# Down-projection of a GeGLU feed-forward by seven block products instead of eight

## The chip, the cores and the metric

The kernel runs on one core of a Trainium2 chip. The metric is the time of one execution on the device in microseconds (us), as the median of several runs. A core has five engines that run side by side, each with an instruction queue of its own: TensorE (PE in the profile; its weight loads are listed apart as PEld), VectorE (DVE), ScalarE (ACT), GpSimd (POOL) and SyncE (SP), which here issues the DMAs. TensorE holds a stationary operand of up to 128x128, streams a moving operand through it, and adds into PSUM, of which a bank holds 128x512 f32. The other operands live in SBUF. [...]

## The reference

One transformer layer: attention against a cached window with 32 query heads, and a feed-forward network (FFN), each with an adaptive layer norm and a gate. x has 2048 rows of 512, the FFN is 1792 wide.

```
mod = (silu(c) @ w_mod).reshape(1, 6, 1, -1)
sa, ca, ga, sb, cb, gb = (mod[:, i] for i in range(6))
h = layernorm(x) * (1 + ca) + sa
x = x + ga * attention(h)
h = layernorm(x) * (1 + cb) + sb
x = x + gb * ((gelu(h @ w_gate) * (h @ w_up)) @ w_down)
```

The last product, `@ w_down`, with its row gate `gb`, is what the change is about: a matrix A = gelu(..) * (..) of 2048x1792 by a matrix of 1792x512.

## The kernel before

**Precision.** Each f32 operand is split into two f16 parts, a high and a low one (`halves`, line 152, on GpSimd: one tensor_scalar and one subtract), and each product is made of three matmuls, high by high, high by low, low by high (`mm3`, line 84; its three matmuls are lines 85, 86 and 87 for every use, so groups are told apart by their tiles). Operands are scaled by powers and norms first, so that f16 holds them.

**Order of the whole.** Attention comes first, in 512 steps t (T = 512) whose order on every engine is written out by hand. In its later half the FFN weights are prepared beside it: loaded, scaled, split and stored to a scratch tensor in HBM (`prep_set` for gate and up, `prep_wd` for down). `sched(pos, (load, steps), ...)` plans a buffer: the load, and at which t its steps run; the buffers of tag `raw` (5) and `rw` (2) turn round. A `store` puts the DMA on SP's queue at the step given. On the same queue go the transposes of p, the softmax output, which attention's product with v needs (`pt<-p`). Then comes the FFN; there only SP's order is written out, and a scheduler chooses the order on the other engines from program order and dependences.

**FFN loops.** The rows are taken in two halves of 1024, each as two blocks of 512. The 1792 features are taken in NP = 7 pairs of 128-wide tiles; n counts pairs over both halves (0 to 13), and q = 2n is the gate, q = 2n + 1 the up product of a pair (NQ = 28). Gate and up are already made by seven block products per q (`product`, line 775; `ORDER` gives their order 1, 2, 6, 7, 5, 4, 3), each of 6 matmuls with a 128x512 moving operand. Their four results are named by (row block, feature tile): `"11"`, `"12"`, `"21"`, `"22"`. For even q, `result` (line 1222) applies gelu; for odd q it multiplies by the up product on VectorE and splits the outcome into f16 parts: a ScalarE copy (line 1230) and a VectorE subtract (line 1231), into tiles of tag `ot`, named `at`.

**Down-projection.** `y_tasks` (line 861) makes one row tile of 128 rows of one pair: two weight tiles x three terms = 6 matmuls with a 128x512 moving operand (the down weights, all 512 columns) and A's parts as stationary operand, into one PSUM bank, tag `acc` (`NACC` = 5 banks, name `py`). VectorE then scales and adds it into the row's accumulator (line 877, `acc<-py,dysc,acc`). Pair n's eight row tiles are queued when q = 2n + 1 is done, and `y_next` takes one after each of four products per q. Each pair's two weight tiles of 256 KB are fetched once per half (line 1504). `f_final` (line 1526) stores a finished row tile and frees its accumulator for one of the second half.

**Weight preparation.** `prep_wd` (line 1316) loads two tiles of w_down, takes a norm, and in `make` multiplies by the row gate (line 1333) and the scale (line 160), splits (lines 156 and 157) and stores two tiles of 256 KB.

## Time and profile before

| what | us |
|---|---|
| median of 3 runs | 1746.65 |
| lowest and highest | 1745.91, 1747.25 |
| the profiled execution, its own time | 1745.58 |
| its span, first to last instruction | 1743.8 |
| VectorE busy over the span | 1467.2 |
| TensorE busy over the span | 1717.1 |
| attention without the FFN's preparation | about 0 to 688 |
| attention with it | about 688 to 1240 |
| the FFN | from about 1240 |

The profile is one execution, recorded by the hardware. Times are in us unless marked ns. A group of instructions is shown with its line, its engine, the operation, what it writes and reads (`out<-in`), the tile's shape, the count, then busy time and the mean duration in ns, and the idle time of the engine just before such instructions, with what ended it. A line of the timeline has the start, the duration, the engine, the line of the kernel, the operation and the count of merged instructions. A line of the waits has the engine and line that waited, what it waited for, the sum in us, how often, and the longest. Records of matmuls overlap: the duration of one holds its way through the array, in which the next has begun.

### The profile page before, as it was taken

The numbers are of one execution on the slowest core, as the hardware profiler recorded it, in microseconds if no ns is written. First come the engines' busy times: TensorE is split into PE (matmuls) and PEld (weight loads), VectorE is DVE, ScalarE is ACT, GpSimd is POOL, SyncE is SP. The second block draws the span as 40 slices with busy tenths as digits, with TensorE's granted clock in tenths as the row PEclk, the third lists the DMA queues.
The fourth block names the chain that finished last, engine by engine and source line by source line (L and its number), as shares of the span: only waits on it lengthen the run. The fifth ranks groups of instructions, "written<-read, shape, count | busy, mean of one in ns | idle before, by whom it ended". The sixth has DMA issues, their size and how long they took to land.

```text
span 1743.8 us, 25747 instructions
## 1 busy us (share of the span) xinstructions
PE 1717.1 (98%) x8002; PEld 783.9 (45%) x8002; DVE 1467.2 (84%) x2544; ACT 1208.9 (69%) x2713; POOL 931.8 (53%) x1137
## 2 busy tenths in 40 slices
PE   7999999999999999999999999999999999999999
PEld 4344444444444444444444444444444444444444
DVE  7888898999988889898898898998875888766676
ACT  6988888888877777688778778788774344434342
POOL 4899768788887844557486486675303323100000
PEclk9999999999999999999999999999999999999999
DMA  6989999999999998899999999999976545352222
GB/s 210 234 190 222 213 229 205 239 215 222 229 197 229 221 202 162 188 213 228 225 209 220 241 213 215 212 223 227 199 160 161 172 113 141 91 190 76 88 76 76
DMA packets 692842, 330.23 MB, mean 189 GB/s; under 512 B 597088, under 2 KB 607584, under 8 KB 692704
## 3 DMA queue, kind: packets, MB, share of 16 engines
q1 hardware_dynamic: 692416, 328.06, 82.5%
q8 instruction: 63, 1.03, 0.3%
q14 instruction: 75, 0.61, 0.1%
q10 hardware_dynamic: 288, 0.52, 0.1%
HBM read 129.63 MB, written 53.61 MB: 105 GB/s over the span
## 4 chain that ended last, share of the span: by engine, by line
PE 88%; DVE 4%; POOL 3%; DMA 2%; ACT 2%; issue 1%; SPq 0%; POOLq 0%; ACTq 0%
PE py L85 9%; PE py L87 9%; PE py L86 9%; PE po L85 6%; PE po L87 6%; PE po L86 6%; PE ps L85 6%; PE ps L87 5%; PE ps L86 5%; PE fa L85 3%; PE fa L86 3%; PE fa L87 3%; PE qa L85 3%; PE qa L87 3%; PE qa L86 3%; DMA pt<-p 2%
## 5 line engine op out<-in xcount | busy, mean ns | idle before, releaser
L929 ACT ACTIVATE ee<-ps,nm 128x512 f32<-128x512 f32 x512 | 350.5, 685 | 243.3 <-DVE nm L920 240.2
L948 DVE SCALAR_TENSOR_TENSOR p<-ee,rr,p 128x512 f16<-128x512 f32 x512 | 456.8, 892 | 2.1 <-ACT p L943 1.9
L920 DVE TENSOR_REDUCE nm<-ps 128x1 f32<-128x512 f32 x512 | 350.4, 684 | 105.1 <-PE ps L87 101.9
L943 ACT ACTIVATE p<-ee,rr 128x512 f16<-128x512 f32 x512 | 363.1, 709 | 10.6 <-DMA pt<-p 9.5
L85 PE MATMUL ps<-k,qt 128*128 128x512 f16 x512 | 193.9, 379 | 5.3 <-ACT ee L929 4.5
L85 PE MATMUL po<-pt,v 128*128 128x512 f16 x512 | 194.0, 379 | 4.1 <-DMA pt<-p 2.4
L87 PE MATMUL po<-pt,v 128*128 128x512 f16 x512 | 194.1, 379 | 1.4 <-POOL v L157 1.4
L87 PE MATMUL ps<-k,qt 128*128 128x512 f16 x512 | 194.0, 379 | 0.6 <-DVE qt L667 0.6
L86 PE MATMUL py<-wo,ot 128*128 128x512 f16 x512 | 194.0, 379 | 0.0
L87 PE MATMUL py<-wo,ot 128*128 128x512 f16 x512 | 194.0, 379 | 0.0
L86 PE MATMUL po<-pt,v 128*128 128x512 f16 x512 | 194.0, 379 | 0.0
L85 PE MATMUL py<-wo,ot 128*128 128x512 f16 x512 | 194.0, 379 | 0.0
L86 PE MATMUL ps<-k,qt 128*128 128x512 f16 x512 | 193.9, 379 | 0.0
L86 PEld LDWEIGHTS <-w 128*128 128x128 f16 x728 | 71.2, 98 | 87.5 <-issue 1.9
L87 PEld LDWEIGHTS <-w 128*128 128x128 f16 x728 | 71.2, 98 | 86.6 <-POOL w L157 0.6
L85 PEld LDWEIGHTS <-w 128*128 128x128 f16 x728 | 71.2, 98 | 86.5 <-DMA w<-kept 1.2
L667 DVE SCALAR_TENSOR_TENSOR ot<-po,ot 128x512 f16<-128x512 f32 x128 | 86.7, 677 | 23.4 <-ACT ot L666 23.4
L877 DVE SCALAR_TENSOR_TENSOR acc<-py,dysc,acc 128x512 f32<-128x512 f32 x112 | 81.3, 745 | 23.8 <-PE py L87 23.1
L929 ACT ACTIVATION_READ_ACCUMULATOR ee<-ps,nm 128x1 f32 x512 | 99.4, 194 | 0.0
L485 POOL TENSOR_TENSOR turn<-xs,turn 128x512 f16<-128x512 f32 (+1 forms) x48 | 57.3, 1195 | 75.5 <-ACT turn L482 75.2
L890 POOL TENSOR_TENSOR acc<-acc,gate 128x512 f32<-128x512 f32 x16 | 24.3, 1516 | 127.9 <-DVE acc L877 127.9
L877 DVE SCALAR_TENSOR_TENSOR acc<-py,ysc,acc 128x512 f32<-128x512 f32 x112 | 82.7, 738 | 10.6 <-PE py L87 10.6
(265 smaller groups left out, 3829.1 us busy)
## 6 DMA issues: line engine op xcount, KB each, us to landing
w<-kept SPq DMA_DIRECT2D x123, 256.0 KB, 3.2
wo<-kept SPq DMA_DIRECT2D x60, 256.0 KB, 3.5
raw<-in_wo SPq DMA_DIRECT2D x56, 256.0 KB, 3.2
kept<-stage SPq DMA_DIRECT2D x56, 256.0 KB, 3.2
kept<-w SPq DMA_DIRECT2D x39, 256.0 KB, 3.1
rw<-in_wq SPq DMA_DIRECT2D x38, 256.0 KB, 3.1
pt<-p SPq DMA_TRANSPOSE x512, 3.4
kept<-wo SPq DMA_DIRECT2D x32, 256.0 KB, 2.9
```

What stands on the lines that cost most here:

```text
L85: nc.tensor.matmul(ps, lhi, rhi, start=first, stop=False, skip_group_check=chain)
L86: nc.tensor.matmul(ps, lhi, rlo, start=False, stop=False, skip_group_check=chain)
L87: nc.tensor.matmul(ps, llo, rhi, start=False, stop=last, skip_group_check=chain)
L485: nc.gpsimd.tensor_tensor(S[s][:, :, 1, :], side(s), S[s][:, :, 0, :], op=ALU.subtract)
L667: return lambda: nc.vector.scalar_tensor_tensor(t[:, 1, :], src, scale, t[:, 0, :], op0=ALU.mult, op1=ALU.subtract)
L877: nc.vector.scalar_tensor_tensor(acc[ti], st["p"], by, acc[ti], op0=ALU.mult, op1=ALU.add)
L890: nc.gpsimd.tensor_tensor(acc[ti], acc[ti], rows[2], op=ALU.mult)
L920: nc.vector.tensor_reduce(nm, E[t]["ps"], axis=AX.X, op=ALU.max, negate=True)
L929: nc.scalar.activation(e, E[t]["ps"], AF.Exp, bias=E[t]["nm"], scale=1.0, accum_out=sm[:, t % 2:t % 2 + 1])
L943: nc.scalar.activation(p16[:, 0, :], E[t]["e"], AF.Copy, scale=E[t]["r"])
L948: nc.vector.scalar_tensor_tensor(p16[:, 1, :], E[t]["e"], E[t]["r"], p16[:, 0, :], op0=ALU.mult, op1=ALU.subtract)
```

## The change

The down-projection too goes by Strassen's seven products (in a form with few additions). For a pair of feature tiles, A's 1024 rows are two blocks of 512 by two tiles of 128, and the down weights are two tiles by two column halves of 256. Seven products of combinations of these replace eight.

- Operands of A (`operands`, new): from the four results, seven f16 pairs F[1] to F[7]. `"11"`, `"22"` and `"12"` are split as before (ScalarE, VectorE); four sums and differences and the splits of four of the operands are done on GpSimd.
- Weights (`prep_wd`): four differences of 128x256 on GpSimd, and 3.5 stored tiles of 256 KB instead of 2. The positions of `prep_set` move by one to three steps.
- `down`: an item is one product k for two row tiles (u) and one or two pairs n. It takes 6 matmuls with a 128x256 moving operand per row tile and pair; two pairs are summed in PSUM (three groups of two pairs and one single pair in each half, 14 items each). Products 1, 6, 7 and 4 add up in one bank of tag `qa`, products 5 and 3 in another, product 2 has its own. After each product VectorE adds the bank into one quarter of the output block, a tile of 128x2x256.
- Each item fetches its own weights, 128 KB per pair, six items ahead, into the eight `wo` buffers.
- `y_step` takes at most one item after a product: at four of seven products of an even q, at three of an odd one, once the group's last pair is ready; at every product for the second half's single pair. The last group of two pairs follows after the loop, with the two row-tile pairs alternating.

```diff
-GU = 2.0 ** -38
+GU = 2.0 ** -39
...
+    def operands(n, key, g):
+        F = A.setdefault(n, {})
+        F[key] = g
+
+        def split(t):
+            nc.scalar.activation(t[:, 0, :], g, AF.Copy)
+            nc.vector.tensor_tensor(t[:, 1, :], g, t[:, 0, :], op=ALU.subtract)
+            return t
+
+        def tt(o, a, b, op=ALU.subtract):
+            nc.gpsimd.tensor_tensor(o, a, b, op=op)
+
+        if key == "11":
+            F[4] = split(pair("ot", "at", NOT))
+        elif key == "22":
+            X = pool.tile([P, 4, 2, 512], F16, tag="pt", name="ax", bufs=NPT)
+            F[1], F[2], F[6], F[7] = (X[:, k] for k in range(4))
+            split(F[1])
+        elif key == "21":
+            tt(F["11"], g, F["11"], ALU.add)
+            tt(g, F["22"], g)
+            tt(F["22"], F["11"], F["22"])
+            halves(F[6], F["22"])
+            halves(F[7], g)
+        else:
+            split(F[2])
+            tt(g, g, F["22"])
+            F[5] = pair("ot", "at", NOT)
+            halves(F[5], F["11"])
+            F[3] = get_v() if n % 2 else get_qt()
+            halves(F[3], g)
...
+        def s1():
+            scaled(1)
+            minus((2, l), (1, r), (1, l))
+            minus((2, r), (0, r), (2, l))
+            minus((1, r), (0, r), (1, r))
+
+        def s3():
+            minus((0, l), (0, l), (2, r))
+            halves(outs[3][0]["t"][:, :, l], st[0][:, l])
...
+        sched(b, (lambda: load(0), [lambda: stat(0), nop]), b + 13)
+        sched(b + 1, (lambda: load(1), [lambda: stat(1), spread, nop]), b + 4, b + 11)
+        sched(b + 7, (outs[0][1], [s0, keep_it(0)]), b + 10)
+        sched(b + 9, (more, [s1, nop]), b + 12)
+        sched(b + 11, (outs[1][1], [lambda: halves(outs[1][0]["t"], st[1]), keep_it(1)]), b + 14)
+        sched(b + 12, (outs[2][1], [lambda: halves(outs[2][0]["t"], st[2]), keep_it(2)]), b + 15)
+        sched(b + 13, (outs[3][1], [s3, keep_it(3)]), b + 16)
...
+    SPOT = {1: (1, 0), 2: (0, 0), 3: (0, 1), 4: (3, 0), 5: (2, 0), 6: (2, 1), 7: (1, 1)}
+    INTO = {1: (1, 0), 2: (1, 0), 6: (1, 1), 7: (0, 1), 4: (0, 0), 5: (0, 1), 3: (1, 1)}
+    YORDER = (1, 2, 6, 7, 4, 5, 3)
...
+    def down(ns, u, k, st, last):
+        box = {}
+
+        def fetch_w():
+            box["w"] = get_wo().rearrange("p a (n c) -> p n a c", n=2)
+            j, side = SPOT[k]
+            for i, n in enumerate(ns):
+                dma(box["w"][:, i], KEPT["wd", n % NP, j][:, :, side * 256:side * 256 + 256])
+
+        def go():
+            key = "a" if k in (1, 6, 7, 4) else "b" if k == 2 else "c"
+            if k in (1, 2, 5):
+                st[key] = (bank("s", "ya", 2) if u and ns[-1] == 2 * NP - 1 else bank("qa", "ya", 1)) if k == 1 else bank("acc", "y" + key, NACC)
+            for r in range(2):
+                ps = st[key][:, r * 256:r * 256 + 256]
+                sl = slice((2 * u + r) * P, (2 * u + r + 1) * P)
+                for i, n in enumerate(ns):
+                    t, w = A[n][k], box["w"][:, i]
+                    mm3(ps, t[:, 0, sl], t[:, 1, sl], w[:, 0, :], w[:, 1, :], r + i == 0 and k in (1, 2, 5), r == 1 and i == len(ns) - 1 and k in (2, 4, 3), True)
+            q, h = INTO[k]
+            flat = facc[q, u, h].rearrange("p r c -> p (r c)")
+            by = col("dmx", (ns[-1] % NP + 1) // 2) if len(ns) > 1 else col("dysc", ns[0] % NP)
+            nc.vector.scalar_tensor_tensor(flat, st[key], by, flat, op0=ALU.mult, op1=ALU.add)
+            if last and k in (2, 3, 4, 5):
+                store_facc(ns[0] // NP, q, u, h)
+
+        return fetch_w, go, len(ns)
+
+    GROUPS = [tuple(NP * half + n for n in ns) for half in range(2) for ns in [(0,)] + [(i, i + 1) for i in range(1, NP, 2)]]
+    for ns in GROUPS:
+        sts = ({}, {})
+        last = ns[-1] % NP == NP - 1
+        if ns[-1] == 2 * NP - 1:
+            order = [(u, k) for k in YORDER for u in range(2)]
+        else:
+            order = [(u, k) for u in range(2) for k in YORDER]
+        queue += [(ns[-1],) + down(ns, u, k, sts[u], last) for u, k in order]
+
+    def prefetch(ahead=6):
+        while done_to[0] < min(len(queue), len(ready) + ahead):
+            queue[done_to[0]][1]()
+            done_to[0] += 1
...
+    def y_step(q, k):
+        if len(ready) < len(queue):
+            n, _, _, cost = queue[len(ready)]
+            full = cost == 1 and n > 0
+            if n <= (q - 2) // 2 and (full or k in ((0, 2, 4, 6), (2, 4, 6))[q % 2]):
+                y_next()
+        prefetch()
...
-            if k in (1, 2, 5, 6) or load_later:
-                y_next()
...
+            if q > 0:
+                y_step(q, k)
+            load_next(q)
```

More of the change, by code (lines that the diff above doesn't have):

```diff
@@ L893, in back, with y1_row @@
         nc.gpsimd.tensor_tensor(acc[ti], acc[ti], XR[ti], op=ALU.add)
+    def y1_row(ti):
+        return y1[ti // 2][ti % 2]
     def keep_row(ti):
-        y1[ti] = dram.tile([P, D], F32, name=f"y{ti}")
-        dma(y1[ti], acc[ti])
+        if ti // 2 not in y1:
+            y1[ti // 2] = dram.tile([2, P, D], F32, name=f"y{ti // 2}")
+        dma(y1_row(ti), acc[ti])
     def attn_final(ti):
@@ L1241, in place @@
             if m == 0:
-                return tmp("fg")
-            return pool.tile([P, QB], F32, tag="p16", name="fu", bufs=NP16) if k == "s1" else kept(k)
+                return pool.tile([P, QB], F32, tag="p16", name="fg", bufs=NP16) if q and k != "s1" else tmp("fg")
+            return kept(k)
         def after(k):
@@ new lines, in block_kernel, with row_pair, load_facc, store_facc @@
+    YORDER = (1, 2, 6, 7, 4, 5, 3)
+    def row_pair(half, q, u):
+        return (2 * half + q) * QT + 2 * u
+    def load_facc(half, q, u, h):
+        facc[q, u, h] = t = pool.tile([P, 2, D // 2], F32, tag="acc", name="acc", bufs=2 * QT)
+        dma(t, y1[row_pair(half, q, u) // 2].rearrange("r p c -> p r c")[:, :, h * 256:h * 256 + 256])
+    def store_facc(half, q, u, h):
+        ti = row_pair(half, q, u)
+        dma(out[ti * P:(ti + 2) * P, h * 256:h * 256 + 256].rearrange("(r p) c -> p r c", p=P), facc[q, u, h])
+        if half == 0:
+            load_later.append((1, q, u, h))
@@ L1538, in block_kernel @@
             run(("f", q, k))
-            if k in (1, 2, 5, 6) or load_later:
-                y_next()
-        if m == 1:
-            for qi, (a, b) in enumerate((("11", "21"), ("12", "22"))):
-                for i in range(QT):
-                    nexty.append(y_tasks((2 * (n // NP) + qi) * QT + i, [lambda n=n, a=a: A[n, a], lambda n=n, b=b: A[n, b]],
-                                         [("f", n, 0), ("f", n, 1)], col("dysc", n % NP), f_final if n % NP == NP - 1 else None))
-    while nexty:
+            if q > 0:
+                y_step(q, k)
+            load_next(q)
+    while len(ready) < len(queue):
+        prefetch()
         y_next()
```

86 lines of the change are left out of this document (45 added, 41 removed).

## The prediction

> **What bounds the kernel now.** I read the page's head first, then the busy times by stretch, then what TensorE waited for.
>
> ```profile
> span 1743.8 us, 25747 instructions
> PE 1717.1 (98%) x8002; PEld 783.9 (45%) x8002; DVE 1467.2 (84%) x2544; ACT 1208.9 (69%) x2713; POOL 931.8 (53%) x1137
> ```
> ```profile
> 688.00:1240.00 552.00, 548.56 (x2565) 249.09 (x2564) 488.76 (x841) 433.30 (x1016) 351.53 (x420) 1.00 0.99 217
> 1240.00:1744.00 504.00, 497.22 (x2301) 224.84 (x2299) 368.64 (x579) 225.49 (x399) 61.14 (x56) 1.00 0.45 126
> ```
> ```profile
> PE ps L85 <- ACT ee L929: 4.5, 7, 1.3
> PE po L85 <- DMA pt<-p: 2.4, 4, 1.4
> ...
> PE po L87 <- POOL v L157: 1.4, 2, 0.8
> PE fa L85 <- ACT u L806: 1.4, 2, 0.7
> ```
>
> The two stretches (columns: width, then PE, PEld, DVE, ACT, POOL busy, the granted clock, the DMA share, GB/s) are the later attention half, in which the FFN weights are prepared, and the FFN itself, the last 504 us. TensorE is busy for 548.6 of 552 and 497.2 of 504 us at clock 1.00, and its waits are a few us in all. So the time is the number of matmuls times their spacing, and only TensorE's own work changes it, so long as nobody else falls behind. A matmul's own duration in these records is no price, because they overlap. The price is start to start. The first and the last of 94 matmuls, in order, with nothing between but their like:
>
> ```profile
> 1349.83 0.38 PE L87 MATMUL py<-wo,ot 128*128 128x512 f16 x1
> ...
> 1369.90 0.38 PE L86 MATMUL fc<-C,w 128*128 128x512 f16 x1
> ```
>
> 93 steps in 20.07 us are **0.2158 us** for a matmul of 512 columns, attention and FFN alike. The records say 0.38.
>
> **The change: the products.** The down-projection of before is these three groups:
>
> ```profile
> L85 PE MATMUL py<-wo,at 128*128 128x512 f16 x224 | 84.9, 379 | 0.0
> L86 PE MATMUL py<-wo,at 128*128 128x512 f16 x224 | 84.9, 379 | 0.0
> L87 PE MATMUL py<-wo,at 128*128 128x512 f16 x224 | 82.4, 379 | 0.0
> ```
>
> 672 matmuls (2 row halves x 7 weight pairs x 8 row tiles x 2 weight tiles x 3 terms) x 0.2158 = **145.0 us**. After: 14 pairs x 7 products x 4 row tiles x 3 terms = 1176 matmuls of 256 columns. The columns fall from 344,064 to 301,056, by an eighth (18.1 us at 0.2158/512 per column), while the instructions rise by 504. So everything hangs on the spacing of a 256-column matmul with a new weight load for each, which the trace does not have. Break-even is 145.0 / 1176 = 0.1233 us. The nearest rows:
>
> ```profile
> 1201.52 0.17 PE L220 MATMUL pst<-lm,ones 128*128 128x2 bf16 x1
> 1201.55 0.38 PE L85 MATMUL ps<-k,qt 128*128 128x512 f16 x1
> ```
> ```profile
> 1201.31 0.10 PEld L220 LDWEIGHTS <-ones 128*128 128x128 bf16 x1
> 1201.53 0.10 PEld L85 LDWEIGHTS <-qt 128*128 128x128 f16 x1
> 1201.55 0.10 PEld L86 LDWEIGHTS <-qt 128*128 128x128 f16 x1
> ```
> ```profile
> 33.24 1.64 PE L421 MATMUL pln<-ident,xb 128*128 128x128 f32 x13 [0.57 <-DVE xb L395]
> ```
>
> A matmul of 2 columns costs its successor 0.03 us, with its own weights and the successor's. Two loads start 0.02 us apart though each lasts 0.10, so loads are pipelined and their 98 ns are no floor for a pair. Lower end: half of 0.2158, 0.108. Upper end: a straight line from 0.03 at 2 columns to 0.2158 at 512, 0.1225 at 256. The 13 transposes of the third fence, each with a load, stand (1.64 - 0.28) / 12 = 0.113 apart, in f32 and 128 columns wide: no like form, but pairs that follow at that rate. I take **0.110**, by half the 512-column step with a little fixed cost: 129.4 us, so **-15.6**. The ends are 127.0 (-18.0) and 144.1 (-0.9).
>
> [...]
>
> **Adding up out of PSUM.** Before: 112 adds `acc<-py`. After: 14 items (2 row-tile pairs x 7 products) for each of 8 weight groups, each with one add of the same 128x512 form: 112 again, because two pairs are summed in PSUM first.
>
> ```profile
> L877 DVE SCALAR_TENSOR_TENSOR acc<-py,dysc,acc x112: 720/745/752, 1368.9 to 1740.0; 128x512 f32<-128x512 f32 x112
> L1231 DVE TENSOR_TENSOR at<-fg,at x56: 674/692/1564, 1337.8 to 1733.7; 128x512 f16<-128x512 f32 x56
> ```
>
> 0 for the adds. What is new is that products 1, 6, 7 and 4 of an item run share one bank: 6 must wait until the add after 1 has read it. Queued behind a waiting matmul stands all of TensorE. Cover: between two items lie mostly two gate/up products, 12 x 0.2158 = 2.6 us, against an add of 0.745 and the lag before it. How long DVE lets a finished product wait:
>
> ```profile
> 1504.80 0.38 PE L87 MATMUL py<-wo,at 128*128 128x512 f16 x1
> ```
> ```profile
> 1505.72 0.75 DVE L877 SCALAR_TENSOR_TENSOR acc<-py,dysc,acc 128x512 f32<-128x512 f32 x1
> ```
>
> 0.54 us after the matmul's end there, so 1.3 us of 2.6 to 3. Uncovered, a step costs 0.745 + the 0.16 by which a matmul's record outlasts its step + about 0.1, near 1.0 us. In the tail the two row-tile pairs alternate, so one item (12 x 0.110 = 1.3 us) lies between: covered, barely. The single pair 7 runs an item in every slot, with one product (1.3 us) between. I put +1 on these two places; ends 0 and +8 (8 dependent steps of 1.0).
>
> **Operands.** Per pair, four splits (ACT copy, DVE subtract) become three, and POOL gets 4 adds/subtracts and 4 splits of two operations: 12 operations of 128x512. Rows:
>
> ```profile
> L156 POOL TENSOR_SCALAR stage<-raw 128x512 f16<-128x512 f32 x14 | 10.3, 736 | 1.2
> L157 POOL TENSOR_TENSOR stage<-raw,stage 128x512 f16<-128x512 f32 x14 | 19.3, 1376 | 1.2
> L893 POOL TENSOR_TENSOR acc<-acc,xr 128x512 f32<-128x512 f32 x16 | 21.7, 1358 | 8.8 <-DMA xr<-in_x 8.2
> L1333 POOL TENSOR_TENSOR raw<-raw,gate 128x512 f32<-128x512 f32 x14 | 20.5, 1462 | 0.3
> L160 POOL TENSOR_SCALAR raw<-raw,dsc 128x512 f32<-128x512 f32 x14 | 13.0, 927 | 2.2 <-DVE dsc L303 0.8
> L1284 POOL TENSOR_TENSOR rw<-rw 128x256 f32<-128x256 f32 x56 | 51.9, 928 | 4.2
> L157 POOL TENSOR_TENSOR stage<-rw,stage 128x256 f16<-128x256 f32 x14 | 9.7, 694 | 1.2
> L156 POOL TENSOR_SCALAR stage<-rw 128x256 f16<-128x256 f32 x14 | 8.3, 595 | 1.2
> ```
>
> 4 x 1.36 + 4 x (0.74 + 1.38) = 13.9 us per pair. A pair of TensorE's work lasts 84 x 0.2158 + 84 x 0.110 = 27.4 us, and POOL is busy for 61 of 504 us there: covered. DVE loses 14 subtracts (9.7 us), but its subtract of two SBUF inputs reaches 1564 ns at its slowest against a median of 692, and POOL's new work makes that likelier; with DVE at 369 of 504 us I price it at 0. The latency is what matters: operand 6 needs five POOL operations (3 x 1.36 + 2.12 = 6.2 us) behind DVE's multiply of 0.7, so about 7.2 us after its product. Within the loop it is used about 10 us after (six products of 1.3 us and two items); in the tail after product 3 (1.3 us) and five items (6.5 us), 7.8: slack of 0.6. There I keep 0 to +3.
>
> **Weights.** Before: 28 fetches of 256 KB in the FFN. After: 28 + 168 = 196 of 128 KB, each product loading its own quarter.
>
> ```profile
> wo<-kept SPq DMA_DIRECT2D x60, 256.0 KB, 3.5
> ...
> kept<-stage SPq DMA_DIRECT2D x56, 256.0 KB, 3.2
> ...
> x<-kept SPq DMA_DIRECT2D x41, 128.0 KB, 2.5
> ```
>
> 25.7 MB for 7.3 over 504 us is +36 GB/s on 126, with a DMA share of 0.45. Six items ahead is 6 x 1.3 = 7.8 us even in the tail, against 3.5. SP stands at a load until a slot's reader is done, two items back, with the next gate/up loads behind it; those are asked for nearly a whole q ahead. 0; if that cover were gone, one load's 3.5 us now and then.
>
> **Preparation in attention.** Each pair's weight preparation goes on POOL from 2 x (1.46 + 0.93 + 0.74 + 1.38) = 9.0 us to 4.8 + 3 full splits (6.4) + 4 half-width subtracts (3.7) + a half-width split (1.3) = 16.1: +50 us over seven pairs, on 351 busy of 552. It also stores 3.5 instead of 2 times 256 KB per pair, 10.5 stores more, at a DMA share of 0.99. TensorE waited 1.4 us for POOL and 2.4 for the transposed p, over the whole run. SP's stores stand ahead of p's transposes, but come three steps (over 7 us) after their split. I put +0.5; ends 0 and +8 (10.5 times half of a 3.2 us landing, half of it reaching TensorE, once per store: 8).
>
> **Sum.** -15.6 + 1 + 0.5 = **-14.1**. The profiled execution took 1745.6 us, span 1743.8 and 1.8 around it, 1.1 below the median 1746.65; on the median that is 1732.5. The last add and store keep their form.
>
> **Rivals.**
> - **The pair is dearer than its columns** (0.1225): a fixed cost of instruction and load adds to the stream. -0.9 + 1.5, no change: 1747. The line through two columns speaks for it, the transposes at 0.113 against it. [...]
> - **The shared bank** (the other side, slower). If the scheduler puts items of one bank next to each other, TensorE stands for the add: 3 dependent steps x 2 row-tile pairs x 8 groups = 48, about 1.0 us each. From 16 exposed steps on it eats the gain; with 40 exposed the time is 1745.6 - 15.6 + 40 + 1, on the median 1772. Against it: the dependence itself now spaces them. For it: items came bunched before. Of the third terms (L87) of a stretch, these are the first and the last of five in a row, 0.65 us apart, all of the down-projection, with no gate/up product between:
>
> ```profile
> 1506.53 0.38 PE L87 MATMUL py<-wo,at 128*128 128x512 f16 x1
> ...
> 1509.12 0.38 PE L87 MATMUL py<-wo,at 128*128 128x512 f16 x1
> ```
>
> - **Attention pays**: POOL and DMA late by the upper end, +8: -15.6 + 1 + 8 = -6.6, on the median 1740. For it DMA at 0.99; against it TensorE's 2.4 us.
> - **It doesn't do what it says**: the columns are counted from the loops, so I leave it no chance.
>
> **How the numbers follow.** Forecast 0.64, attention or the tail costing half 0.14, dear pairs 0.12, the bank 0.10. The measurement tells 0.2%, 3.5 us, from no change. Faster 0.78, same 0.12, slower 0.10. Prediction 1732.5. The range runs from the lower end of the pair with no stall, 1746.65 - 18.0 = 1728.6, less 1.5 of the few us that TensorE now idles in the FFN, 1727, to the dear pair, 1747; the bank's case stays outside.
>
> **What would show it.** Matmuls of 256 columns 0.108 to 0.113 apart; the last 504 us about 15 shorter, the stretch before as long as it was; no wait of the new product line for DVE's add or POOL's operands above 2 us in all. Wrong if the pairs stand 0.12 apart, if TensorE's idle in the FFN grows beyond 10 us, or if waits for p's transposes grow in attention.

## The result and the profile after

The changed kernel takes **1771.76 us** (median of 5 runs, 1765.86 to 1774.68), the kernel before 1746.65 beside it: a ratio of 1.0135, with a 95% interval of 1.0115 to 1.0155. It is 25.1 us slower, where 14.1 us less was forecast, and lies outside the range. The profiled execution took 1774.68 us, the slowest of the five, so the shares read from it below add up to its own 29.1 us and not to 25.1. One of the ten runs of `e13_prep_no_pool` below took 2004.08 us at a granted clock of 0.852 and is left out of its median. The page's head:

```profile
span 1772.9 us, 27282 instructions
...
PE 1713.0 (97%) x8504; PEld 834.6 (47%) x8506; DVE 1495.6 (84%) x2533; ACT 1197.6 (68%) x2699; POOL 1179.1 (67%) x1370
```

TensorE is busy for 4.1 us less than before (1713.0 against 1717.1) while the span is 29.1 longer: for the most part it stands still. But its busy time should have fallen by 15.6. A part of the difference is slower running: the mean granted clock of this run is 0.994, of the kernel before 1.00, and the last section estimates that at 9 us. The busy times by stretch, with the columns as before:

```profile
688.00:1240.00 552.00, 542.84 (x2519) 245.64 (x2518) 484.46 (x831) 425.23 (x1000) 387.94 (x470) 0.99 1.01 217
1240.00:1773.00 533.00, 499.74 (x2851) 279.74 (x2849) 400.85 (x577) 222.28 (x401) 271.81 (x240) 0.99 0.59 159
```

Before, TensorE idled 3.4 and 6.8 us in these two; now 9.2 and 33.3. GpSimd's busy time in the last stretch has gone from 61.1 to 271.8, 211 more, where 195 was counted (14 x 13.9). What TensorE waited for:

```profile
PE fa L85 <- DMA w<-kept: 8.8, 4, 3.7
PE ps L85 <- ACT ee L945: 7.9, 9, 2.9
...
PE fa L85 <- ACT fg L818: 4.0, 3, 1.7
PE ya L85 <- DVE acc L1598: 3.7, 4, 1.9
PE ya L87 <- POOL ax L157: 3.0, 2, 2.8
PE yc L85 <- DVE acc L1598: 2.6, 2, 1.6
...
PE fa L85 <- DVE fg L1265: 2.2, 1, 2.2
```

No wait is large. There are many small ones of four kinds: weights (`w<-kept`), attention's scores waiting for ScalarE (`ps`), gate and up results late on ScalarE and VectorE (`fg`), and the down-projection's banks (`acc`) and operands (`ax`). The last score matmul marks the end of attention (count, shortest/median/longest in ns, first to last start); after, then before:

```profile
L85 PE MATMUL ps<-k,qt x512: 376/379/473, 24.7 to 1324.2; 128*128 128x512 f16 x171
```
```profile
L85 PE MATMUL ps<-k,qt x512: 376/379/390, 24.8 to 1314.2; 128*128 128x512 f16 x171
```

Attention ends 10.0 us later, and what follows takes 448.7 us (1772.9 - 1324.2) instead of 429.6: 19.1 more. The matmuls themselves do what was forecast. In the timeline, the first and the last of the twelve of one item of two pairs (an item has three for each row tile and pair; the six in the list of the change are of both row tiles):

```profile
1689.64 0.27 PE L85 MATMUL ya<-wo,ax 128*128 128x256 f16 x1
...
1690.85 0.27 PE L87 MATMUL ya<-wo,ax 128*128 128x256 f16 x1
```

11 steps in 1.21 us are 0.110. So the question is where 15.6 gained and 25.1 lost, some 41 us, stand.

### The profile page after: what moved, and what is told of

Same layout as the page of the kernel before. It is cut to its first block, busy times and chain, and to the rows that moved or that the text cites. A ratio compares the mean times of both kernels' runs of the same rounds, so it can differ in the third digit from the quotient of the medians.

```text
span 1772.9 us, 27282 instructions
## 1 busy us (share of the span) xinstructions
PE 1713.0 (97%) x8504; PEld 834.6 (47%) x8506; DVE 1495.6 (84%) x2533; ACT 1197.6 (68%) x2699; POOL 1179.1 (67%) x1370
## 4 chain that ended last, share of the span: by engine, by line
PE 74%; POOL 9%; DVE 7%; DMA 4%; ACT 3%; issue 2%; SPq 1%; POOLq 0%; ACTq 0%
PE py L86 5%; PE py L85 5%; PE py L87 5%; PE po L87 5%; PE po L85 5%; PE po L86 5%; PE ps L85 5%; PE ps L87 5%; PE ps L86 5%; PE qa L85 3%; PE qa L86 3%; PE qa L87 3%; PE fa L85 2%; PE fa L87 2%; PE fa L86 2%
## 5 line engine op out<-in xcount | busy, mean ns | idle before, releaser
L964 DVE SCALAR_TENSOR_TENSOR p<-ee,rr,p 128x512 f16<-128x512 f32 x512 | 464.3, 907 | 4.2 <-ACT p L959 4.0
L1220 POOL TENSOR_TENSOR fg<-fg 128x512 f32<-128x512 f32 x56 | 80.8, 1443 | 127.2 <-DVE fg L1276 122.1
L889 DVE SCALAR_TENSOR_TENSOR acc<-py,ysc,acc 128x512 f32<-128x512 f32 x112 | 82.7, 739 | 10.6 <-PE py L87 10.6
L85 PEld LDWEIGHTS <-v 128*128 128x128 f16 x540 | 52.9, 98 | 66.8 <-issue 5.5
```

The costliest lines, as they stand in the source:

```text
L85: nc.tensor.matmul(ps, lhi, rhi, start=first, stop=False, skip_group_check=chain)
L889: nc.vector.scalar_tensor_tensor(acc[ti], st["p"], by, acc[ti], op0=ALU.mult, op1=ALU.add)
L964: nc.vector.scalar_tensor_tensor(p16[:, 1, :], E[t]["e"], E[t]["r"], p16[:, 0, :], op0=ALU.mult, op1=ALU.subtract)
L1220: nc.gpsimd.tensor_tensor(o, a, b, op=op)
```

## The experiments

The theory: three costs, each priced near nothing, in three places: GpSimd's preparation in attention, its operand work in the FFN, and the order and fetches of the down-projection's items. The rivals: SP's positions and load slack (attention), and the fetches or the banks alone (FFN). All runs, each with the before of its own chip; "excess" is one median less the other.

| run | median us | before | excess | ratio, 95% interval |
|---|---|---|---|---|
| the change | 1771.76 | 1746.65 | +25.1 | 1.0115 to 1.0155 |
| e1_prep_alone | 1754.70 | 1745.73 | +9.0 | 1.0033 to 1.0063 |
| e13_prep_no_pool | 1744.03 | 1745.67 | -1.6 | 0.9981 to 1.0003 |
| e2_slack | 1767.84 | 1745.73 | +22.1 | 1.0112 to 1.0142 |
| e7_prep_pos | 1775.29 | 1746.92 | +28.4 | 1.0144 to 1.0177 |
| e3_no_pool | 1754.03 | 1745.73 | +8.3 | 1.0025 to 1.0054 |
| e12_pool_unread | 1763.65 | 1745.67 | +18.0 | 1.0081 to 1.0125 |
| e5_act_copies | 1768.01 | 1746.92 | +21.1 | 1.0106 to 1.0136 |
| e4_one_dma | 1767.88 | 1745.73 | +22.2 | 1.0109 to 1.0140 |
| e8_interleave | 1760.19 | 1746.92 | +13.3 | 1.0064 to 1.0098 |
| e11_share | 1754.76 | 1745.67 | +9.1 | 1.0032 to 1.0062 |
| e9_best | 1766.36 | 1746.92 | +19.4 | 1.0094 to 1.0134 |
| e10_old_pos | 1779.16 | 1745.67 | +33.5 | 1.0161 to 1.0216 |
| e14_lean | 1752.87 | 1746.29 | +6.6 | 1.0023 to 1.0048 |
| e15_closed | 1729.76 | 1746.29 | -16.5 | 0.9897 to 0.9923 |

A difference of two excesses carries both intervals, about 0.25%, 4 us; smaller ones are not read.

### Attention

**The preparation alone.** The kernel before, with the change's `prep_set`, `prep_wd` and scales, and its own FFN.

```diff
-        outs = [staged() for _ in range(2)]
+        outs = [staged() for _ in range(4)]
...
+        sched(b + 9, (more, [s1, nop]), b + 12)
+        sched(b + 11, (outs[1][1], [lambda: halves(outs[1][0]["t"], st[1]), keep_it(1)]), b + 14)
+        sched(b + 12, (outs[2][1], [lambda: halves(outs[2][0]["t"], st[2]), keep_it(2)]), b + 15)
+        sched(b + 13, (outs[3][1], [s3, keep_it(3)]), b + 16)
```

> The kernel before with the change's weight preparation (positions, GpSimd operations, stores) and the FFN of before, which reads two of the stored tiles as its down weights; the output is therefore not the layer's. Theory (attention part is lost on its own: SP's load of an up-weight tile waits for the split that frees its buffer, so ScalarE's statistic of it waits, and TensorE behind ScalarE): 5 to 10 us over before, 1752 to 1757, with TensorE waits on ScalarE's exponential and statistic between 900 and 1250 us. Rival (all of the loss is made in the FFN, the attention part was chance or is paid back): within 2 us of 1746.6.

+9.0 us, with the last score matmul at 1323.4 and 430.1 us behind it, as before. So attention's loss is made by the preparation, without the new FFN. In six other kernels below that have this same preparation (e3, e4, e5, e8, e11, e12) the last score matmul starts between 1319.9 and 1323.9, so a single profile gives this loss only to some 4 us.

**The preparation without GpSimd's added work.** As above; the four differences and the splits of two tiles are gone, and the second tile is stored in their place, with the same stores at the same steps.

```diff
             scaled(1)
-            minus((2, l), (1, r), (1, l))
-            minus((2, r), (0, r), (2, l))
-            minus((1, r), (0, r), (1, r))
...
-        sched(b + 12, (outs[2][1], [lambda: halves(outs[2][0]["t"], st[2]), keep_it(2)]), b + 15)
-        sched(b + 13, (outs[3][1], [s3, keep_it(3)]), b + 16)
+        def again(k):
+            return lambda: store(("wd", n, k), outs[1][0]["t"] if k < 3 else outs[1][0]["t"][:, :, l], 0)
...
+        sched(b + 11, (outs[1][1], [lambda: halves(outs[1][0]["t"], st[1]), keep_it(1), again(2), again(3)]), b + 14, b + 15, b + 16)
```

> The run with the change's preparation alone and the FFN of before, without the down preparation's extra GpSimd work: its four differences and the splits of the third and fourth tile are left out, and the second tile is stored in their place, so that the stores are as many and of the same size; the gate and up sets stand at the change's positions. If GpSimd's added work makes the attention part late: back to 1746 to 1748. If the positions or the stores do: 1752 to 1757 as with that work.

No loss is left (-1.6 us). So neither the 10.5 further stores nor the moved positions cost anything here; GpSimd's added 6.8 us per pair do (in the changed kernel it is busy for 480.0 us between 560 and 1325 us, before for 432.5), together with the buffers that this work fills (three of tag `raw` per pair, which the edit leaves free too; they were not tried apart). The same stretch in the two kernels, with the preparation whole and then without that work:

```profile
688.00:1240.00 552.00, 543.77 (x2524) 246.14 (x2523) 484.85 (x833) 425.34 (x1001) 387.85 (x470) 0.99 1.01 217
```
```profile
688.00:1240.00 552.00, 549.60 (x2569) 249.87 (x2568) 488.64 (x845) 432.50 (x1018) 355.39 (x429) 1.00 1.02 221
```

TensorE idles 8.2 us instead of 2.4. The chain of waits of the changed kernel shows the way there at one stall (start, duration, what):

```profile
1061.65 1.17 POOL stage L157
1062.82 0.02 issue
1062.84 2.83 DMA rw<-in_wu
1065.67 0.02 issue
1065.69 0.72 ACT junk L216 x2
1066.42 0.67 ACT ee L945 x2
...
1067.13 0.38 PE ps L85
...
1068.90 0.43 PE po L85
1069.33 0.43 PE po L86
```

GpSimd's split ends late; only then is the `rw` buffer free, and SP, which stood at that load, issues it 0.02 us later. The load takes 2.83 us. ScalarE has the statistic of that tile (`junk`) as its next instruction and stands before it, with softmax (`ee`) queued behind; TensorE's next scores wait 2.91 us for `ee`. GpSimd isn't named in TensorE's wait. The same chain, split, load, statistic, stands in front of two more stalls, with the splits at 923.53 and 1200.73. Over the later attention half ScalarE waits 19.8 us for loads of up tiles (`rw<-in_wu`); before it was 1.7, without GpSimd's added work it is 9.1.

**More room, other positions.** Rival: the loads are asked for too early or too late. 28 steps per pair instead of 27, and the up tiles one step later; then 28 steps with before's positions of `prep_set`.

```diff
-        b = T // 2 + 30 + 27 * n
+        b = T // 2 + 30 + 28 * n
...
-        prep_set(2 * n + 1, b + 13)
+        prep_set(2 * n + 1, b + 14)
```

> The changed kernel with the preparation spread out by one step per pair: a pair every 28 steps instead of 27, the up set 14 steps after the gate set instead of 13. Nothing else. Theory: the up tiles are loaded one step earlier before their statistic, the three stalls between 900 and 1250 us go, the last score matmul returns from 1324 to about 1315, and the time falls by 6 to 10 us to about 1763. Rival (GpSimd or the DMA engines are short in attention, whatever the spacing): the stalls move, time within 3 us of 1771.8.

```diff
-        sched(b + 1, (lambda: set_load(key, srcs, 0), [lambda: pair_stat(key, m, 0), nop]), b + 11, kind="rw")
+        sched(b, (lambda: set_load(key, srcs, 0), [lambda: pair_stat(key, m, 0), nop]), b + 9, kind="rw")
...
-        b = T // 2 + 30 + 27 * n
+        b = T // 2 + 30 + 28 * n
```

> The changed kernel with the gate and up preparation back at its positions of before and a pair every 28 steps instead of 27; the new down preparation stays. Theory (the change's later positions left the up tile's load one step short of its statistic; GpSimd's and the DMA queue's added work are not the cause): the stalls behind ScalarE's statistic go, the last score matmul starts by 1317 instead of 1324, time about 1764. Rival (the extra GpSimd work and stores in attention cost it, wherever the gate and up sets stand): other stalls come in their place, as in the run with 28 steps and one step more between the sets, and the last score matmul stays at 1321 or later.

The first gains 3.0 us, less than such a difference can show: the waits of `ps` for `ee` fall from 7.9 to 4.3, those for the transposed p rise from 2.3 to 6.8. Other waits come in place of the stalls. The second is not better (+28.4), and attention ends at 1331.2. What was expected of the two by their theories, an end of attention by 1315 and 1317, did not come: neither touches GpSimd's work.

### The operands in the FFN

**Without GpSimd's operand work.** Products 3, 5, 6 and 7 read operands 2, 4, 1 and 1; their sums and splits are left out, all matmuls stay.

```diff
-            tt(F["11"], g, F["11"], ALU.add)
-            tt(g, F["22"], g)
-            tt(F["22"], F["11"], F["22"])
-            halves(F[6], F["22"])
-            halves(F[7], g)
+            F[6], F[7] = F[1], F[1]
...
-            tt(g, g, F["22"])
-            F[5] = pair("ot", "at", NOT)
-            halves(F[5], F["11"])
-            F[3] = get_v() if n % 2 else get_qt()
-            halves(F[3], g)
+            F[5], F[3] = F[4], F[2]
```

> The changed kernel without GpSimd's operand work in the FFN: the four sums and the four splits on GpSimd are left out, and products 3, 5, 6 and 7 read the operands of 2, 4, 1 and 1 instead. All matmuls, adds and fetches stay. Theory (GpSimd's work lengthens DVE's operations with two SBUF inputs, and DVE's lag is what TensorE waits for, and in the tail GpSimd itself): the gelu operations of DVE return from 0.88 and 0.82 to about 0.735 us, the waits on DVE, ScalarE and GpSimd in the FFN (about 20 us with the slow clock after them) go, time 1748 to 1754; the waits for gate and up weights (about 9 us) stay. Rival (the FFN's loss is SyncE's queue): DVE gets shorter, but the time falls by less than 6 us.

+8.3 instead of +25.1: **16.8 us** hang on work that was priced at 0. TensorE's waits for the down-projection's banks, 6.3 us in the changed kernel (3.7 + 2.6), shrink to one:

```profile
PE ya L85 <- DVE acc L1590: 0.3, 1, 0.3
```

Between 1325 and 1775 us VectorE is busy for 303.8 us there against 334.3, with the same 462 instructions. The groups of VectorE in that stretch, of the changed kernel:

```profile
L1258 DVE SCALAR_TENSOR_TENSOR sq<-sq,fg 128x512 f32<-128x512 f32 x42 | 37.1, 884 | 15.0 <-ACT sq L1255 14.6
...
L1265 DVE SCALAR_TENSOR_TENSOR fg<-sq,fg 128x512 f32<-128x512 f32 x42 | 34.5, 821 | 9.2 <-ACT sq L1261 8.5
...
L1265 DVE SCALAR_TENSOR_TENSOR fg<-sq,fa 128x512 f32<-128x512 f32 x14 | 9.5, 681 | 1.2 <-ACT sq L1261 1.2
...
L1258 DVE SCALAR_TENSOR_TENSOR sq<-sq,fa 128x512 f32<-128x512 f32 x14 | 9.5, 676 | 0.6 <-ACT sq L1255 0.6
```

and of the kernel without that work:

```profile
L1250 DVE SCALAR_TENSOR_TENSOR sq<-sq,fg 128x512 f32<-128x512 f32 x42 | 29.0, 691 | 14.9 <-ACT sq L1247 14.8
L1257 DVE SCALAR_TENSOR_TENSOR fg<-sq,fg 128x512 f32<-128x512 f32 x42 | 28.8, 686 | 10.0 <-ACT sq L1253 9.3
```

The fence of the changed kernel holds its own control. The same line with `fa`, a PSUM bank, as second input takes 676 to 681 ns; with `fg`, a tile in SBUF, 821 to 884, and 686 to 691 without GpSimd's operand work. One such pair in the timeline of the changed kernel, and the same instruction some us later:

```profile
1411.24 1.70 POOL L1220 TENSOR_TENSOR fg<-fg 128x512 f32<-128x512 f32 x1
...
1411.74 1.75 DVE L1258 SCALAR_TENSOR_TENSOR sq<-sq,fg 128x512 f32<-128x512 f32 x1
...
1417.71 0.68 DVE L1258 SCALAR_TENSOR_TENSOR sq<-sq,fg 128x512 f32<-128x512 f32 x1
```

VectorE's slow instruction begins 0.50 us after GpSimd's, which has two SBUF inputs too, and ends 0.55 us after its end (1413.49 against 1412.94). The later one takes 0.68 although GpSimd's `turn<-xs,turn`, also of two SBUF inputs, starts with it at 1417.7; there GpSimd's is the long one, 1.66 us where the one before it took 1.16. What decides which of the two is lengthened was not shown.

Why this reached TensorE: 369 busy of 504 us was a mean. 1400 to 1500, where the second half's layer norm runs beside the FFN, in the kernel before, the changed one, and the one without operand work:

```profile
1400.00:1500.00 100.00, 100.00 (x465) 45.32 (x464) 87.13 (x137) 46.01 (x75) 31.39 (x30) 1.00 0.45 124
```
```profile
1400.00:1500.00 100.00, 88.42 (x521) 50.46 (x518) 92.54 (x125) 39.01 (x65) 81.93 (x72) 1.00 0.63 168
```
```profile
1400.00:1500.00 100.00, 94.57 (x557) 54.61 (x556) 84.42 (x135) 47.18 (x77) 30.99 (x30) 0.98 0.69 174
```

VectorE (third busy figure) was already at 87 of 100 there. Changed, it is at 92.5 and does fewer instructions (125 for 137); TensorE loses 11.6 us in these 100, and without the operand work 5.4. (The two later kernels are some 10 us behind the first in the program, so the work in the stretch is not quite the same.) All six waits for banks lie between 1426 and 1489 us. Before the longest, 1.90 us, VectorE's add began at 1431.76, 6.6 us after the bank's last matmul had ended at 1425.13, behind two-input instructions of 1.3 to 1.75 us; the prediction had read a lag of 0.54.

**The work done, the operands not read.** GpSimd does all of it, but products 3, 5, 6 and 7 read 2, 4, 1 and 1.

```diff
-                    t, w = A[n][k], box["w"][:, i]
+                    t, w = A[n][{3: 2, 5: 4, 6: 1, 7: 1}.get(k, k)], box["w"][:, i]
```

> The changed kernel with all of GpSimd's operand work, but products 3, 5, 6 and 7 read the operands of 2, 4, 1 and 1, so that nothing waits for GpSimd's results and only its work beside DVE stays. Theory (GpSimd slows DVE's operations with two SBUF inputs, and that is what costs): most of the 17.7 us of the run without this work is still lost: 1764 to 1771, with DVE's gelu operations at 0.82 to 0.90 us. Rival (late operands are what costs, directly and through the items' order): 1753 to 1758.

+18.0. Of the 16.8 us, 9.7 are then GpSimd's mere running (18.0 - 8.3), and 7.1 operands that come late (25.1 - 18.0), each to about 4 us. That the running costs through VectorE is what the trace suggests: TensorE still loses 12.9 us between 1400 and 1500, with VectorE busy for 92.8, and VectorE's two groups stay slow:

```profile
L1258 DVE SCALAR_TENSOR_TENSOR sq<-sq,fg 128x512 f32<-128x512 f32 x42 | 37.4, 891 | 13.3 <-ACT sq L1255 13.1
L1265 DVE SCALAR_TENSOR_TENSOR fg<-sq,fg 128x512 f32<-128x512 f32 x42 | 37.0, 882 | 10.2 <-ACT sq L1261 9.3
```

**Half of GpSimd's splits to ScalarE.** The high copies of operands 3, 5, 6 and 7.

```diff
-            halves(F[6], F["22"])
-            halves(F[7], g)
+            halves(F[6], F["22"], True)
+            halves(F[7], g, True)
...
-            halves(F[5], F["11"])
+            halves(F[5], F["11"], True)
...
-            halves(F[3], g)
+            halves(F[3], g, True)
```

> The changed kernel with the high parts of operands 3, 5, 6 and 7 copied by ScalarE instead of GpSimd (the subtracts for the low parts stay on GpSimd): 56 GpSimd operations of about 0.85 us fewer, 56 ScalarE copies of about 0.63 us more. Theory (GpSimd's FFN work is what costs the 17.7 us that leaving it out gave back, through DVE's two-input operations and through late operands): a fifth of GpSimd's operand time goes, operand 6 comes one hand-over earlier, time down by 3 to 8 us to about 1766. Rival (only GpSimd's two-input subtracts and sums disturb DVE): DVE's means unchanged, time within 2 us of 1771.8.

+21.1: 4 us, at the edge of what can be told, so inconclusive. VectorE's two groups stay at 897 and 800 ns: what is taken away has one input, and the instructions of two inputs stay.

### The items' order and fetches

SP's own queue in the timeline of the changed kernel, near one of the waits for `w`:

```profile
1574.28 0.41 SPq L93 DMA_DIRECT2D out_y<-acc  x1
1574.80 1.23 SPq L93 DMA_DIRECT2D wo<-kept  x2
1576.08 0.65 SPq L93 DMA_DIRECT2D acc<-y  x1
1576.82 1.18 SPq L93 DMA_DIRECT2D wo<-kept  x2
1578.05 0.60 SPq L93 DMA_DIRECT2D w<-kept  x1
```

Each issue holds SP for 0.4 to 0.65 us. The 168 further fetches are some 100 us of SP (168 x 0.6, an estimate), and the gate and up loads stand in the same line.

**One DMA for an item's two pairs.** The stored tiles of two pairs lie together; 112 issues instead of 196.

```diff
-            for i, n in enumerate(ns):
-                dma(box["w"][:, i], KEPT["wd", n % NP, j][:, :, side * 256:side * 256 + 256])
+            src = KEPT["wdp", (ns[-1] % NP + 1) // 2, j]
+            if len(ns) == 2:
+                src = src.rearrange("p k n c -> p k (n c)")
+                dma(w, src[:, side::2, :] if j < 3 else src)
```

> The changed kernel with both pairs' quarter weights side by side in the scratch tensor, so that an item of two pairs is fetched by one DMA of 256 KB instead of two of 128 KB: 112 issues on SyncE's queue in the FFN instead of 196, the same bytes. Theory (SyncE's queue is late: about 0.6 us for each issue, and loads for gate and up queue behind): the waits of the gate and up products for their weights, 9.4 us in the profile, fall under 3, time down by 6 to 9 us to about 1764. Rival (the loads are late because SyncE waits for accumulators and slots, not for its own issue time): the waits stay within 3 us of 9.4 and the time within 3 us of 1771.8.

+22.2, 2.9 less: not to be told from nothing. Of its waits:

```profile
PE ya L85 <- DVE acc L1611: 13.3, 8, 5.1
...
PE fa L85 <- DMA w<-kept: 2.3, 2, 1.4
```

Those for `w` fall from 8.8 to 2.3, those for product 1's bank rise from 3.7 to 13.3. A reading that fits, but is not shown: weights that come earlier let the items run closer, and they meet in the shared bank. The rival of the expectation, that SP is late because it stands at slots, is not borne out: between 1325 and 1775 us it stands for 124.9 us at `wo` slots still being read, against 92.8 in the changed kernel, and the gate and up weights come earlier all the same.

**The two row-tile pairs in turn.** The order of the tail, in all groups.

```diff
-                st[key] = (bank("s", "ya", 2) if u and ns[-1] == 2 * NP - 1 else bank("qa", "ya", 1)) if k == 1 else bank("acc", "y" + key, NACC)
+                st[key] = bank("qa", "ya", 1) if k == 1 and not u else bank("acc", "y" + key, NACC)
...
-        if ns[-1] == 2 * NP - 1:
-            order = [(u, k) for k in YORDER for u in range(2)]
-        else:
-            order = [(u, k) for u in range(2) for k in YORDER]
+        order = [(u, k) for k in YORDER for u in range(2)]
```

> The changed kernel with the two row-tile pairs alternating in every group, not only in the last, and the second pair's first bank taken from the five common ones. Two items of one bank then have another item between them always; matmuls, fetches and operands are the same. Theory (TensorE waits for DVE's add because the products 1, 6, 7 and 4 share a bank): the waits of ya and yc on DVE's add, 6.3 us in the profile, fall under 1.5, time down by 4 to 8 us to about 1766. Rival (DVE's lag is in all its work; the wait goes over to the gate and up products): the sum of TensorE's waits on DVE and ScalarE in the FFN, 13 us, stays above 10 and the time within 3 us of 1771.8.

+13.3: **11.8 us less**, by the order and the second bank that it needs. Two items of one bank are now an item apart, and an operand is needed later. Of its waits:

```profile
PE yc L85 <- DMA wo<-kept: 4.5, 1, 4.5
```

The bank's wait has sunk to 0.7, and no wait for `w` is named any more; a late `wo` in the tail is the largest of the FFN now.

**Order and fetch together.** Both, and since two items in turn use the same weights, one fetch for both: 56 issues.

```diff
         def fetch_w():
-            box["w"] = get_wo().rearrange("p a (n c) -> p n a c", n=2)
+            if u:
+                return
+            w = get_wo()
...
-    def prefetch(ahead=6):
+    def prefetch(ahead=10):
```

> The changed kernel with alternating row-tile pairs in every group, both pairs' weights by one DMA and fetched once for the two row-tile pairs (56 issues instead of 196), up to ten items ahead; GpSimd's copies and the preparation as in the change. Theory (alternating the pairs took the waits for adds and for gate and up weights away; what is left is DVE behind GpSimd, and a late fetch in the tail): 4 to 6 us under the 1760 of alternating alone, by the 4.5 us wait for a late fetch in its tail: about 1755. Rival (the fetches no longer matter): 1758 to 1762.

+9.1: **16.0 us less** than the change. No `wo` wait is left. Behind the last score matmul it takes 432.6 us instead of 448.7.

### Put together

Two kernels took this FFN with the ScalarE copies of e5 and another preparation: `e9_best` before's positions of `prep_set` at 28 steps per pair (as in e7), `e10_old_pos` the same at 27.

```diff
-        b = T // 2 + 30 + 28 * n
+        b = T // 2 + 30 + 27 * n
```

> Everything together: ScalarE copies for operands 3, 5, 6 and 7; alternating row-tile pairs; both pairs' weights by one DMA, fetched once for the two row-tile pairs of a product and up to ten items ahead (56 issues instead of 196, half the bytes); the preparation at its positions of before with a pair every 28 steps. If the three causes are independent and each is mostly removed, the attention part returns to within 3 us of before and the FFN gains 10 or more on it: 1733 to 1742. If GpSimd's remaining subtracts hold DVE back all the same: 1745 to 1755.

> The run with everything together, but with a pair every 27 steps as in the change, and the gate and up preparation at its positions of before. Theory (28 steps per pair, not the positions of before, made the attention part worse there: the loads fall on other steps of the attention's own loads and stores): the last score matmul starts by 1322, as in the changed kernel, or earlier, and the time is 1748 to 1756. Rival (the positions of before don't go with the longer down preparation): the last score matmul starts after 1328, time above 1758.

Both miss: +19.4 and +33.5. In e9_best the FFN is short, 432.0 us from the last score matmul to the end, but attention ends at 1337.3; in the other at 1341.8. Moving the loads back to before's positions, with GpSimd's new work still there, makes attention longer, as in e7, at 27 steps per pair as at 28.

**The shared fetch with a lighter GpSimd in attention.** To e11_share, ScalarE makes the high copies of two weight tiles, and the second half's layer norm starts its blocks further apart.

```diff
-        sched(b + 11, (outs[1][1], [lambda: halves(outs[1][0]["t"], st[1]), keep_it(1)]), b + 14)
+        sched(b + 11, (outs[1][1], [lambda: halves(outs[1][0]["t"], st[1], True), keep_it(1)]), b + 14)
...
-        b = 26 + 16 * i
+        b = 26 + 18 * i
```

> A try at a faster full version: alternating row-tile pairs with one shared fetch, the high parts of the second and third down-weight tile copied by ScalarE instead of GpSimd in the preparation, and the second half's layer norm spread over the FFN at every 18th product instead of every 16th. Against the same without the last two (1754.8): if GpSimd's added 7 us per pair in the attention matter in proportion, 1.5 us fewer give back 1 to 3 us, and the thinner layer norm 1 to 3 in the stretch where DVE is full: 1748 to 1753. Rival: ScalarE, on which the scores wait, is late by the added copies: 1756 or more.

+6.6, the lowest of the versions that do the whole computation, though 2.5 under e11_share is less than can be told. None of them beats the kernel before.

**The account closed.** e11_share without GpSimd's operand work (as in e3) and without its added preparation (as in e13); all 1176 matmuls, 112 adds and the order stay.

> All three suspected causes taken away at once: alternating row-tile pairs with one shared fetch per product; no operand work on GpSimd in the FFN (products 3, 5, 6 and 7 read the operands of 2, 4, 1 and 1); no extra GpSimd work in the down preparation (its four differences and the splits of the third and fourth tile are left out, the second tile is stored in their place). The 1176 matmuls, the adds and the stores are all there. If the matmuls are worth what they were priced at and these three causes are the whole loss: 1746 less 15 or 16, 1729 to 1734. If something else eats the gain: 1738 or more.

**-16.5 us.** Its stretches:

```profile
688.00:1240.00 552.00, 550.31 (x2573) 250.24 (x2572) 490.34 (x845) 433.24 (x1020) 354.35 (x429) 1.00 1.03 222
1240.00:1773.00 533.00, 478.82 (x2796) 273.38 (x2794) 359.77 (x563) 213.62 (x382) 62.85 (x56) 1.00 0.48 129
```
```profile
L85 PE MATMUL ps<-k,qt x512: 376/379/390, 24.6 to 1312.3; 128*128 128x512 f16 x171
```

With its span of 1727.4 the FFN takes 415.1 us, 14.5 less than before. That is the gain of the cheaper product, as it is when nothing stands against it; a kernel that computes the layer can't leave these operands out. From the change to this kernel it is 41.6 us (25.1 + 16.5); the three parts by themselves were 10.6 (e1 less e13), 16.8 (e3) and 16.0 (e11), together 43.4. They overlap a little: the waits for banks are gone in e3 as well as in e8.

## Why the prediction was wrong

- **Products, -15.6: right.** 0.110 us was taken, 0.110 measured, and e15_closed shows it in the time. "The pair is dearer than its columns" is refuted.
- **Operands, 0: this step failed most.** The prediction had the row (1564 ns at the slowest) and named the danger, then wrote "with DVE at 369 of 504 us I price it at 0". The share was a mean over 504 us; where the second half's layer norm runs, 87 of 100 were taken. GpSimd's busy time, priced rightly, was set against GpSimd's own idle time, while VectorE's two-input instructions paid (884 and 821 ns against 691 and 686). Measured 16.8, of which about 9.7 by GpSimd's mere running and 7.1 by late operands.
- **Latency of operand 6 in the tail, 0 to +3: too small.** The slack of 0.6 us was counted as if the operand's five operations ran one behind the other. In the tail GpSimd runs without a gap from 1741.85, with the split of operand 5 (1.05 and 1.16 us) and the difference for operand 3 (1.27) in between, and the low parts of operands 6 and 7 follow from 1750.54 to 1752.81. The first is done some 10 us after VectorE's multiply, where 6.2 was counted. TensorE waits 1.05 and 2.84 us, and then runs at half rate (last section).
- **Shared bank, +1: mis-sized.** The cover was set against a lag of VectorE of 0.54 us; with GpSimd at work it reached 6.6. Waits of 6.3 us for banks stand in the profile (3.7 + 2.6), nearly all of them gone without GpSimd's operand work (0.3), so this term failed with the one above. The other order is worth 11.8, by more than these waits; which others it saves stays open. The rival "shared bank" gave 1772, and 1771.76 came; but its mechanism, 40 exposed steps of 1.0 us, is not what the trace has, and its number is met by chance.
- **Weights, 0: failed.** Bandwidth and landing times were priced, SP's time per issue (0.4 to 0.65 us) was not. "Those are asked for nearly a whole q ahead" did not hold with 196 issues in the queue: 8.8 us for `w`. Alone, cheaper fetches gave no gain that can be told (e4); with the order they did. How much of the 16.0 is the fetches' own stays open (e11 less e8: 4.2).
- **Attention, +0.5: about the upper end, +8, came (9.0 in e1), by another way.** The bound was worked out from stores, and in e13 the same stores cost nothing that can be told (-1.6). GpSimd was dismissed because TensorE waited only 1.4 us for it; but it reaches TensorE over a buffer, a load and ScalarE's order (2.91 us at the stall shown).
- **The clock, not in the sum.** The stalls were followed by stretches at half rate (granted clock 0.50 to 0.52), an estimated 9 us of the profiled run, spread over the terms above.

The signs named beforehand served: pairs at 0.110, yet the FFN's idle time above 10 us (33.3) and waits for operands above 2 (3.0 for `ax` in the list).

## What to carry to other kernels

An operation moved to an idle engine can be paid for by another one, as here by VectorE: price it on VectorE's two-SBUF-input instructions (800 to 897 ns here in the runs with GpSimd's operand work, 686 to 691 without it), in the busiest stretch of 50 to 100 us, not in a mean (here 87 of 100 us, where the mean was 369 of 504). Count the issues on a DMA queue as well as its bytes (0.4 to 0.65 us of SP each in this case), and what stands behind them. An engine that TensorE isn't seen to wait for can still hold it up through the buffer that it frees late (2.91 us at one stall here). And short stalls that stand close together can cost more than their own length: here stretches at a clock of 0.50 to 0.52 followed five times, an estimated 9 us.

## What the runs showed of the hardware

**In the changed kernel a TensorE that had stood still much ran at half rate afterwards, for 3.4 us at a time and once for 6.8.** In its tail, with the idle time and its releaser in brackets:

```profile
1752.87 0.40 PE L87 MATMUL ya<-wo,ax 128*128 128x256 f16 x1 [2.84 <-POOL ax L157]
1753.05 0.42 PE L85 MATMUL ya<-wo,ax 128*128 128x256 f16 x1
...
1757.53 0.32 PE L87 MATMUL yc<-wo,at 128*128 128x256 f16 x1
1757.69 0.27 PE L85 MATMUL yc<-wo,at 128*128 128x256 f16 x1
```

From 1753.05 to 1757.53 lie 21 steps of 0.213, 0.16 to the next, and 0.27 for a record again. So the 2.84 us of idle time were followed by a further loss of 2.2 us (21 x 0.104). In the chain of attention's stall the last two `po` rows stand 0.43 apart instead of 0.22. It happens five times in this run; two of them by busy times, each with the 3.4 us before the clock falls and the 3.4 after (columns as before):

```profile
1064.60:1068.00 3.40, 0.87 (x5) 0.39 (x5) 0.17 (x1) 2.28 (x7) 1.58 (x2) 1.00 1.04 239
1068.00:1071.40 3.40, 3.40 (x11) 1.27 (x10) 2.75 (x5) 3.26 (x8) 0.00 (x0) 0.52 1.13 230
1580.00:1583.40 3.40, 1.20 (x7) 0.39 (x5) 0.86 (x2) 0.60 (x1) 3.32 (x4) 1.00 0.90 286
1583.40:1586.80 3.40, 3.40 (x10) 1.21 (x9) 0.53 (x1) 1.21 (x2) 0.61 (x1) 0.52 0.99 330
```

In the 3.4 us up to 1068.0, 1208.0, 1378.6, 1583.4 and 1750.7 TensorE is busy for 0.87, 1.41, 1.06, 1.20 and 1.67; then the granted clock is 0.50 to 0.52, four times for 3.4 us and in the tail for 6.8. The 3.4 us from 1426.5 and the next 3.4, with TensorE busy for 1.52 and 1.50, had no such sequel (clock 1.00), so no threshold can be read from this run. Four times 3.4 x 0.48 and the 2.2 of the tail are, as an estimate, 9 us of the 29.1 by which this run is longer. The kernel before has a mean of 1.00 over its run.

TensorE was not idle for the whole of any of the five 3.4 us before the clock fell: it was busy for a quarter to a half of the time (0.87 to 1.67 us) and ran at half rate all the same. What lowers the clock, and what sets the length of the stretches, was not shown. Over the five runs of the changed kernel the mean granted clock goes from 0.993 to 0.998, highest in the fastest, so that may be part of why they lie 8.8 us apart. That cause was not tried by itself.
